# Batch 1's queries in one piece of 1024 rows, the first quarter's last links in halves with PSUM banks of their own, and a new order of all steps

## The chip, the core and the metric

The kernel runs on one core of a Trainium2 chip. A core has a matrix engine (PE, with its weight loads shown as PEld), a vector engine (DVE), a scalar engine (ACT), a general engine (POOL) and SP, which here only issues DMAs. Each engine works through its own queue in order. On-chip memory is SBUF (128 partitions) and PSUM, the matrix engine's output memory: eight banks of 512 float32 per partition. The metric is the time of one execution in device microseconds.

## The reference

Four batches of four heads, 1088 rows, head width 32; all inputs float32 except for the sketch matrices and the weights, which come as float64 words.

```python
phi(x) = outer(S1 x, S2 x)                     # 8 x 8 = 64 features per row and head
kv = phi(k)^T v ;  z = sum over rows of phi(k)
x  = (phi(q) kv) / (phi(q) z + 1e-6)           # attention, 4352 x 128 after the heads are joined
a, b = x @ w1, x @ w2                          # 128 -> 1024
out = ((a * b) @ w3) @ w_out                   # 1024 -> 1024 -> 128
```

The last two products are folded: the kernel forms w3 @ w_out (1024 x 128) once and applies that.

## The kernel before

**Steps and an order written out by hand.** `make_steps` defines 964 named steps, each a few instructions on one engine. The string `ORDER` lists all of them, and the last loop of the kernel runs them in that order and chains every engine's instructions (and all DMAs) to it. So each engine's queue is ORDER, cut down to that engine. `POOL` and `ACTS` name the steps that go to POOL or ACT; those in neither run on DVE where the step has a choice. `SLOTS` gives the buffer that each new tile takes: all PSUM tiles come from eight banks of kind "b", and raw weights from three buffers "raw" of 8 KB per partition.

**Keys** (steps `k0` to `k3`, one per batch). `load`, `loadr` bring a batch of k in (the last 64 rows apart), `max`, `g` find a scale, `lead` and `rest` split k into a leading part and the rest (L176/L177 on ACT or L179 on DVE, L600), `gram0` to `gram4` multiply (L608), and from the Gram matrix come `Gm`, `Gt`, `Ga`, `Gb`, `T0`, `T1`, `Ta`, `Tb`, `Ts`, `N0`, `N1`, `Na`, `Nb`, small steps on PE and DVE in turn. `N` gives the coefficients that the queries of the batch need. `ab`, `kp`, `kv`, `kq` form phi(k) and the batch's kv matrix.

**Queries.** `q0` and `q1` are the two halves of batch 0 (`q_part`; `q0` is the first quarter, kind "A"), `q2`, `q3` the halves of batch 1 (`q_wide` with 512 rows), `q4` and `q6` whole batches 2 and 3 (`q_wide` with 1024 rows), `qr` the last 64 rows of all batches. `q_wide` goes: `tr`, `max`, `l2`, `l1`, `rm` (transpose and split), `C0`, `A0`, `C1` on PE into four PSUM banks (L1303, L1294), `At`, `Ct` back to SBUF, then `sm`, `st`, `sh`, `sl`, `sc`, `al`, `p01`, `p2`, `p12`, `dn`, `de`, `rc` for the denominators, `bs`, `phi`, `pT`, then `x` on PE (L1417, four banks) and `xT`. A piece of 512 rows takes phi and pT from buffers of their own; a piece of 1024 takes them from two of the three "raw" buffers, which raw weights use too. In `q_part` of kind "A" the last links come in halves: `x0`, `x1` on PE, `xs0`, `xs1` on DVE, `xt0`, `xt1` on PE, `xT0`, `xT1` on ACT.

**Weights.** `w0`, `w1` bring w1 and w2 (two blocks of 512 columns), `w2` w_out, `w3` to `w10` the eight blocks of w3. Each goes load, `c`, `m` (ACT), `j` (DVE), `a0`, `a1` (POOL, L447 or L444). `f0` to `f7` fold a block of w3 into w_out: `t` on DVE, `m` on PE (L480), `o` on ACT.

**The two big products.** For each of eight groups `g` of 512 rows and each chunk `c` of 128 columns: `a` (L1458) and `b` (L1468) on PE, `c` copies a on ACT, `m` multiplies on DVE, `o` (L1481) sums over the chunks on PE; `gr` is the group of the last rows. `oT` and `st` turn and store a group.

**Warm-ups.** 29 steps `warm0` to `warm28` are 72 matmuls on zeros (L223), placed by ORDER among the others; nobody reads what they write.

Of the kernel before, what the change touches and what calls it, by code (L numbers as in the profile page):

```python
# [54 lines left out]
    k0.Nf k0.Nh k0.Nl k0.kp1 k1.kp0 k1.kp1 k2.kp0 k2.kp1 k2.rest0 k3.kp0 k3.kp1 k3.rest0 q0.p01 q0.p12  # L55
    q0.p2 q0.sca q0.scy q1.phi q2.al q2.bs q2.p01 q2.p12 q2.p2 q2.sc q3.p01 q3.p12 q3.p2 q3.phi0 q3.sc
    q4.al q4.p01 q4.p12 q4.p2 q6.al q6.p01 q6.p12 q6.phi1 q6.sc qr.sc s.Pp s.blk s.blkh s.rest
# [26 lines left out]
q3.C0 q3.A0 q3.C1 g0.4m g1.5m k2.kT1 q3.Ct q3.At k1.kvc w9.c g0.1ab w4.a0 w2.a0 w2.a1 f0.m g1.6a q4.max g0.1am q2.p01
q2.p2 q2.p12 q2.dn w4.a1 q4.l2 g1.6c q2.de k2.Ta g1.1a q2.rc g0.1ba g1.1b kr1.ab g1.4a g1.1c q2.bs g1.4c g0.1bc w9.m
kr1.abc k1.kqt f1.t k2.Tb q2.phi0 g1.4b f1.m k2.Ts q2.pT0 g1.1m k1.kq q2.x0 w9.j k2.N0 k2.N1 q4.l1 f0.o g1.4m k2.kT0
q3.sm g1.0o q3.st q2.xT0 g1.6b g2.5a q3.sh k2.Na k2.Nr q3.sl g1.2b g2.5c f1.o w9.a0 q3.sc warm15 q3.p01 v2.zero k2.ab
g1.6m k2.Nb q3.al q3.p2 q4.rm v2.load w6.load q4.C0 q4.A0 q4.C1 g1.2m k2.abt g2.5b w6.m w6.c g2.7a q4.Ct g0.1bb warm14
w5.load w7.load g2.0a w5.c g2.7c w7.c q4.At g1.1o g2.2b w9.a1 q3.p12 g0.1bm w7.m q3.dn q3.de w6.j g2.5m q3.rc w7.j
q3.bs q3.phi0 w5.j g2.2a g2.3a q3.load k3.load v2.loadr k3.loadr g2.3c g2.2c w7.a0 k3.max f6.t q4.sm g2.2m q4.st  # L90
q3.pT0 w7.a1 g2.4a g2.0b g2.6a w8.load f6.m g2.6c g2.0c w8.c g1.3b g1.3m k3.g g2.4c g2.7b g0.0o f6.o w8.m w8.j w8.a0
w10.load g2.0m w8.a1 q3.x0 q3.xT0 w5.m f4.t f5.t g2.1a g1.6o warm11 g2.1c k3.lead0 g2.1b g2.3b w5.a0 w5.a1 g2.3m f2.t
g2.7m g2.4b f5.m kh3.load f5.o w10.m f2.m f2.o w10.c w6.a0 g3.6a q4.sh g3.3a g0.1o w6.a1 f3.t q6.tr w10.j f3.m g3.7a
k3.kT0 k2.kp1 g2.1m f4.m w10.a0 g3.3c g3.7c f3.o q4.sl g0.2o g0.6o warm27 g0.3o warm26 g0.5o q4.sc k3.rest0 k2.kp0
g2.4m q4.al q4.p01 q4.p2 kr1.kp k3.gram0 f4.o k3.gram1 k2.kv0 k2.kv3 k2.kv1 k2.kv2 k3.gram2 k2.kvr k3.gram3 w10.a1
k3.gram4 k3.kT1 k3.ab q4.p12 q4.dn q3.restT k2.kvc k2.kqt k2.kq g3.1a g2.0o g0.4o k3.Gm k3.abt v3.zero f7.t g2.6b
g2.6m f7.m k3.kp0 q4.de q4.rc qr.max q4.bs k3.Gt f7.o k3.Ga v3.load v3.loadr g3.2a g0.7o g1.3o g1.4o g2.4o k3.Gb g2.6o
q6.max g3.0a g2.5o g1.5o g1.2o q4.phi0 q4.phi1 k3.kp1 k3.kv0 g0.oT q4.pT0 k3.kv1 q6.l2 q6.l1 q4.pT1 g3.2c g3.1c g3.0c
q6.rm g3.6c qr.l2 k3.kv3 k3.kv2 k3.T0 k3.T1 k3.Ta k3.kvr q4.x0 q4.x1 k3.Tb k3.N0 k3.Ts k3.N1 k3.Na k3.kvc k3.Nb q4.xT0
q4.xT1 g3.3b g2.3o g2.2o q6.C0 k3.Nr q6.A0 q6.C1 q6.At q6.Ct q6.sm q6.st q6.sh q6.sl q6.sc q6.p01 q6.al g4.6a g4.6c  # L100
g2.1o g1.7o g3.4a g2.7o g5.1b g5.3a k3.kqt g5.1a g3.3m qr.l1 g3.4c g4.0a g3.7b g2.oT g4.0c g5.1c g5.1m q6.p2 g3.4b
g4.5a g3.4m qr.rm g5.2a q6.p12 q6.dn q6.de g3.1b g5.5a k3.kq g5.3c g4.5c g3.1m q6.rc g5.5c g5.5b g5.7a g5.0a g5.5m
q6.bs q6.phi0 g4.1a g3.5a g3.7m g1.oT q6.pT0 g4.1c g5.0c g5.6a g5.7c g5.2c g3.0b g3.6b q6.phi1 q6.pT1 g3.6m q6.x0
q6.x1 g5.4a g3.0m g5.6c q6.xT1 g7.5a g4.0b g5.7b g7.5c q6.xT0 g5.4c g4.0m g6.4a g6.4c qr.C0 qr.A0 qr.C1 qr.At qr.sm
g3.5c qr.st g3.0o g5.2b g4.2a qr.sh qr.sl qr.Ct qr.sc g3.2b g3.4o g3.5b qr.al g4.7a g6.7a qr.p01 g3.2m qr.p2 g6.7c
g4.2c g0.st g3.3o qr.p12 g6.6a g5.4b g3.1o g5.0b g4.7c g5.4m qr.dn g3.5m g5.0m g4.3a g6.5a g7.2a g7.6a qr.de g6.5c
g7.6c g3.6o g7.3a g5.7m qr.rc qr.bs g5.3b g3.2o g3.5o g4.7b g5.2m g7.3c g6.6c g5.3m g7.2c g6.0a g4.3c g5.6b g5.0o
g6.0b g3.7o g3.oT qr.phi0 g4.5b g6.7b g6.2a g6.0c g5.6m g4.5m g7.6b g5.1o g5.2o g7.6m g4.7m g5.4o qr.pT0 qr.x0 g5.3o
g5.5o g6.2c qr.xT0 g7.5b gr.7a gr.0a gr.6a gr.0c gr.7c g6.7m g3.st g6.0m g7.5m g4.6b g7.0a g4.6m gr.6c g4.1b g5.6o
gr.4a gr.4c gr.4b gr.4m g4.4b g4.4a g4.4c g7.0c c.act g7.0b gr.5a gr.5c gr.5b g7.0m g4.1m g4.4m gr.5m g4.2b g6.3b  # L110
g6.1b gr.7b gr.7m g4.0o g6.1a g6.1c g4.3b g6.1m g4.4o g6.3a g6.4b g6.4m g4.3m g6.5b g5.7o g5.oT g4.2m g7.4b g7.1a
g7.2b g6.3c g6.6b g6.6m g7.1b g4.1o g7.2m g6.3m gr.1a g7.3b g7.3m gr.3a gr.1c g7.1c g4.2o g4.5o gr.6b g4.6o g4.3o
g4.7o g7.1m g4.oT g6.5m gr.2b g7.4a g6.2b gr.2a g7.4c g7.7a gr.2c gr.2m gr.0b gr.6m g6.2m g7.4m gr.3c g4.st g5.st
# [1465 lines left out]
```

## Time and profile before

| what | value |
|---|---|
| median of 3 runs | 252.19 us (252.1 to 252.4) |
| the profiled execution | 252.42 us, of which its span is 250.5 us |
| PE busy | 245.4 us, 98% of the span |
| DVE busy | 160.0 us (64%), 9 tenths or more in most slices up to 100 us |
| ACT, POOL busy | 100.2 us, 82.0 us |
| granted PE clock | 9 tenths or more in every slice |

All times below are microseconds from the start of the profiled execution's span. The busy share of PE counts the warm-up matmuls too. A matmul of float32 is two records. Durations overlap, since matmuls are pipelined: what a matmul costs the queue is the distance from its start to the next one's, not its own length (a 128x512 matmul record is 0.59 us long, and the next starts 0.43 us after it).

### The profile page before, as it was taken

To read this page: it belongs to the slowest core of one execution; us is meant where nothing else is said; L and a number is where in the kernel's file an instruction comes from. 1 tells how busy PE (TensorE), PEld (TensorE's weight loads), DVE (VectorE), ACT (ScalarE), POOL (GpSimd) and SP (SyncE) were. 2 spreads that over 40 slices of the span, in tenths; PEclk is the share of its full clock that TensorE was granted. 3 is DMA by queue.
4 is the path that set the end of the run, shared out by engine and by line. 5 is a ranking of instruction groups with operands and counts; after the bars stand their busy time and mean duration, and the time that the engine had idled before them with its cause. 6 is when DMAs were issued, how large, how long until landed. Compare 5 with 4: busy or idle time off the path is not lost.

```text
span 250.5 us, 6030 instructions
## 1 busy us (share of the span) xinstructions
PE 245.4 (98%) x2511; PEld 139.9 (56%) x2511; DVE 160.0 (64%) x351; ACT 100.2 (40%) x186; POOL 82.0 (33%) x111
## 2 busy tenths in 40 slices
...
GB/s 184 183 193 329 270 166 175 211 238 237 137 270 235 129 86 0 3 33 61 39 5 3 0 0 4 1 0 3 0 35 7 3 0 0 0 0 84 22 106 63
DMA packets 31131, 22.02 MB, mean 88 GB/s; under 512 B 21248, under 2 KB 25600, under 8 KB 30976
## 3 DMA queue, kind: packets, MB, share of 16 engines
...
q10 hardware_dynamic: 688, 0.59, 0.8%
q8 instruction: 20, 0.33, 0.6%
...
## 4 chain that ended last, share of the span: by engine, by line
PE 92%; DVE 3%; DMA 2%; issue 1%; SPq 1%
PE a_ps L1458 24%; PE b_ps L1468 24%; PE ps_o L1481 22%; PE ps_w3o L480 6%; PE ps_g L608 3%; PE ps_x L1417 2%; PE ps_ac L1303 2%; DMA qh<-in_q_dram 2%; PE ps_kv L718 2%; PE ps_or L1488 1%; PE idle_ps L223 1%; PE ps_xt L1199 1%; PE ps_ab L676 1%; DVE k_m L182 1%; PE ps_kq L754 0%
## 5 line engine op out<-in xcount | busy, mean ns | idle before, releaser
L1474 DVE TENSOR_TENSOR ab<-ffa,b_ps 128x512 f32<-128x512 f32 (+1 forms) x74 | 45.9, 636 | 44.3 <-PE b_ps L1468 34.7
L1463 ACT COPY ffa<-a_ps 128x512 f32<-128x512 f32 (+1 forms) x74 | 38.6, 555 | 86.6 <-PE a_ps L1458 80.9
L1468 PE MATMUL b_ps<-xT,w 128*128 128x512 f32 (+1 forms) x148 | 67.4, 560 | 0.0
L1458 PE MATMUL a_ps<-xT,w 128*128 128x512 f32 (+1 forms) x148 | 66.8, 561 | 0.0
L1481 PE MATMUL ps_o<-ab,w3o 128*128 128x512 f32 x128 | 60.9, 595 | 0.0
L1468 PEld LDWEIGHTS b_ps<-xT,w 128*128 128x128 f32 x148 | 27.4, 190 | 27.9 <-issue 23.4
L1458 PEld LDWEIGHTS a_ps<-xT,w 128*128 128x128 f32 x148 | 27.1, 190 | 27.6 <-issue 22.1
L1481 PEld LDWEIGHTS ps_o<-ab,w3o 128*128 128x128 f32 x128 | 23.8, 190 | 26.0 <-issue 24.3
L444 POOL TENSOR_TENSOR w3c<-cv_c,cv_m 128x512 int32<-128x512 int32 x16 | 20.3, 1281 | 12.5 <-DVE cv_c L433 8.8
L1497 DVE STREAM_TRANSPOSE oT<-ps_o 128x512 f32<-128x512 f32 x8 | 5.7, 713 | 18.7 <-PE ps_o L1481 18.7
L480 PEld LDWEIGHTS ps_w3o<-wo,w3T 128*128 128x128 f32 x128 | 15.4, 192 | 2.9 <-issue 2.2
L480 PE MATMUL ps_w3o<-wo,w3T 128*128 128x128 f32 x128 | 15.4, 275 | 0.0
L1350 POOL TENSOR_TENSOR s_hl<-s_hl,ay_C 128x256 f32<-128x256 f32 (+2 forms) x4 | 3.2, 794 | 37.1 <-DVE s_hl L1346 25.8
L223 PE MATMUL idle_ps<-zeros 128*128 128x256 bf16 x72 | 12.9, 312 | 1.0 <-DVE zeros L195 1.0
L419 ACT ACTIVATE cv_m<-raw 128x1024 int32<-128x1024 uint32 x11 | 13.1, 1188 | 0.0
L231 ACT ACTIVATE cv_c<-raw 128x1024 f32<-128x1024 f32 x11 | 12.9, 1185 | 0.0
L626 POOL TENSOR_TENSOR kp<-kabt 128x1024 f32<-128x1024 f32 x6 | 12.1, 2024 | 1.9 <-DVE kabt L694 1.2
L474 DVE STREAM_TRANSPOSE w3T<-w3c 128x1024 f32<-128x1024 f32 x8 | 9.8, 1223 | 1.0 <-POOL w3c L444 1.0
L223 PEld LDWEIGHTS <-zeros 128*128 128x128 bf16 x72 | 7.8, 111 | 4.0 <-issue 1.3
L1398 POOL TENSOR_TENSOR ph<-s_al,s_bs 128x1024 f32<-128x1024 f32 x2 | 5.1, 2560 | 9.2 <-DVE s_bs L1388 9.2
L1428 ACT COPY xT<-ps_x 128x128 f32<-128x128 f32 (+2 forms) x20 | 4.7, 323 | 8.6 <-PE ps_x L1417 8.6
L608 PE MATMUL ps_g<-kk 128*32 128x64 f32 x288 | 7.8, 224 | 0.2 <-DVE kk L600 0.2
...
## 6 DMA issues: line engine op xcount, KB each, us to landing
...
```

Source lines behind the costliest of these rows:

```text
L223: pe.matmul(t, zeros, bview(zeros, [[0, 2], [1, 128]]), start=True, stop=True)
L231: act.activation(dst, hi.bitcast(F32), ACT.Prelu, scale=2.0 ** -112, alpha=-2.0 ** 32)
L419: act.mul(x["m"], words(0).bitcast(U32), 2.0 ** -29)
L444: pool.tensor_tensor(d, c, m, ALU.add)
L480: pe.matmul(t["o"], w3T[ko][:, c], wo[:, c], start=c == 0, stop=c == NC - 1)
L608: pe.matmul(o[h * D:(h + 1) * D], lhs, rhs, start=start, stop=stop, skip_group_check=True)
L626: eng.tensor_mul(dst, bview(av, [list(av.ap[1]), list(av.ap[2]), [0, r]]), bview(bv, [list(bv.ap[1]), [0, r], list(bv.ap[2])]))
L1458: pe.matmul(x["a"][:, :w], w_of(0, c), xT[g][:, c0:c0 + w], start=True, stop=True)
L1463: act.copy(x["s"][:, :w], x["a"][:, :w])
L1468: pe.matmul(x["b"][:, :w], w_of(1, c), xT[g][:, c0:c0 + w], start=True, stop=True)
L1474: dve.tensor_mul(ab_sb[g, c][:, c0:c0 + w], x["s"][:, :w], x["b"][:, :w])
L1481: pe.matmul(o_ps[g], w3o[:, c], ab_sb[g, c], start=c == 0, stop=c == NC - 1)
```

## The change

Batch 1's queries are one piece of 1024 rows: the steps of `q3` go, those of `q2` work on twice the columns and get second halves (`phi1`, `pT1`, `x1`, `xT1`). So `q2`'s phi and pT now sit in two of the three "raw" buffers. In `q_part` of kind "A", the halves of `x` and of `xt` get a PSUM tile each instead of sharing one. ORDER, POOL and SLOTS are new throughout. 32 steps change between DVE and POOL, among them `q1.phi`, `k3.kp0`, `k3.kp1`, `k0.Nf` to DVE and `q0.phi1`, `q0.al`, `q1.p01`, `q1.p2`, `q1.p12`, `q4.phi0`, `q4.phi1` to POOL. The diff, with ORDER up to batch 2's Gram matmuls and its end, and without POOL and most of SLOTS:

```diff
 SLOTS = {
...
-    "raw": "012101021010210",
+    "raw": "01210120120120120",
...
 ORDER = """
-c.zeros c.ident s.load s.four warm13 k0.zero warm12 warm10 warm9 warm7 k0.load0 k0.loadr k0.load1 q0.load k2.zero
-c.mask s.words k0.max0 kr0.load k0.max1 s.pair k0.max2 s.lead s.low k0.g k0.lead0 warm1 k0.tr1 k0.tr0 warm0 s.sum
-k0.lead1 q0.tr kr0.tr s.rest warm18 k0.rest0 s.T s.tc k0.gram0 s.R k0.gram1 k0.rest1 k0.gram2 k0.gram3 k0.gram4 s.zero
-s.c s.blkh s.blk k1.zero q0.max s.P warm22 q1.tr q0.l2 k0.Gm k0.Gt k0.kT0 k0.Ga k0.Gb w1.load k2.loadr q0.l1 s.Pc
-k0.T0 s.Pm q1.max q0.restT k0.T1 q0.rm k0.Ta kr0.kT k0.kT1 warm4 warm3 k0.ab0 q0.A0 k0.ab1 k0.Tb kr0.ab s.Pp k1.load
-k1.loadr k0.Ts q0.C0 k0.abc0 k0.kp0 k0.N0 k0.N1 k1.max warm24 k0.abc1 q0.sma k0.kp1 k1.tr1 k0.Na k0.Nh kr0.abc k1.tr0
-q1.l2 k1.g v0.zero v0.load warm2 q0.sta k0.Nb k0.Nl q0.sha q0.C0t k1.kT1 q1.l1 q0.A1 k0.kv0 k0.kv3 k0.Nf q0.C1 k0.kv1
-v0.loadr k0.kv2 kr0.kp q0.smy q0.sla k1.lead0 q0.sty q1.rm kr1.load q0.shy k0.kvr warm21 q0.sca q0.p01 q0.al q1.C0
-q0.sly q0.C1t k0.kvm q0.phi0 k0.Nr k0.kzt k2.load q0.phi1 k1.kT0 k0.kz q0.pt0 k1.rest0 q1.A0 warm8 q1.sm kr1.tr q0.pc0
-q0.pt1 w0.load q0.x0 q0.pc1 w0.c q1.st q0.scy q0.p2 q0.p12 s.RC q1.load q0.dn q0.x1 q1.sh q0.de w0.j q0.rc k1.gram0
-q0.xs0 q0.xs1 k1.gram1 k1.gram2 k1.gram3 w0.m q1.sl k1.gram4 warm19 k1.Gm k0.kvc q0.xt0 q1.restT q1.sca k2.max w0.a0
-q0.xt1 w0.a1 warm16 q1.p01 q1.scy k1.Gt warm5 warm17 warm6 s.AR q1.al q1.p2 q1.p12 q1.dn w1.c q0.xT0 q1.de g0.0aa
-q0.xT1 g0.3a g0.2a kr1.kT g0.2c g0.0ac w1.m g0.3c w2.load s.KS k1.Ga k2.g w1.j g0.3b g0.0ab w1.a0 g0.2b g0.0ba k1.T0
-k1.Gb k1.T1 k1.ab q1.rc q1.bs g0.0bc k0.kqt k2.lead0 q3.tr g0.0am g0.2m k1.abt k1.Ta g0.0bb g0.7a g0.4a q1.phi g0.4c
-g0.7c k1.Tb k1.Ts q3.max g0.3m w1.a1 g0.5a q1.pt0 q1.pt1 g0.5b g0.6a k2.rest0 q3.l2 q3.l1 g0.5c q2.tr q2.max q2.l2
-g0.6c q1.pc0 k1.N0 k1.N1 k2.gram0 k2.gram1 k2.gram2 k2.gram3 k1.kp1 k1.kp0 q1.pc1 k2.gram4 warm23 k1.Na g0.5m w3.load
...
-gr.1b g7.4o g2.st g7.2o gr.1m g7.7m gr.3m g7.3o g7.1o g7.7o gr.0o1 gr.6o1 gr.6o0 gr.5o0 g7.oT gr.1o0 gr.5o1 gr.1o1
-gr.4o1 gr.3o1 gr.2o1 g7.st gr.7o1 gr.4o0 gr.3o0 gr.2o0 gr.7o0 gr.oT0 gr.oT1 gr.st1 gr.st0 warm25 warm20 warm28
+c.mask k2.zero c.ident k0.zero s.load c.zeros k0.loadr k0.load0 k0.load1 k0.max0 warm0 k0.tr1 k0.max1 warm14 warm13
+s.words s.pair warm7 warm19 q0.load s.lead warm10 warm1 warm3 k0.max2 s.low k0.g s.sum s.rest k0.lead0 k0.lead1 warm4
+s.P s.T s.tc q0.restT q1.tr k0.rest0 k0.rest1 s.four k0.gram0 k0.gram1 k0.gram2 k0.gram3 k0.gram4 q0.tr q0.max s.Pm
+k0.Gm s.R s.c s.Pc k0.Gt k0.Ga s.blk k0.Gb k0.tr0 k0.kT0 q0.l2 q1.max warm2 k0.T0 kr0.load k0.T1 k0.Ta q0.l1 k0.kT1
+k0.ab0 k0.abc0 k1.zero s.zero s.blkh kr0.tr v0.zero s.Pp w1.load k2.loadr kr0.kT q1.l2 warm22 k0.Tb k0.Ts k1.load
+k0.N0 k0.N1 q0.rm k0.Na q0.A0 k0.ab1 q0.C0 v0.load k0.kp0 k1.tr0 k0.Nh k0.abc1 q1.l1 q0.A1 k1.kT0 q0.C0t q0.sma
+v0.loadr k1.loadr warm23 warm17 kr0.ab k0.kp1 k1.tr1 warm15 q0.sta kr1.load warm16 k0.kv0 k1.max k0.kv3 q0.sha kr0.abc
+k0.Nb kr0.kp k1.g k0.Nf q0.sla k2.load w0.load k0.kv1 k0.kv2 k0.Nl k0.kvr q0.C1 q0.sca k1.kT1 k1.lead0 q1.rm q0.al
+q0.smy k0.kvm q1.A0 q1.C0 s.KS q0.C1t q0.sty q0.phi0 q0.pt0 q1.sm q0.phi1 warm18 warm26 warm8 k0.kzt q0.pt1 kr1.tr
+q0.pc0 q0.shy k1.rest0 k0.kz q0.x0 w0.c k1.gram0 k1.gram1 k1.gram2 k1.gram3 k1.gram4 q1.st q0.pc1 q0.sly q0.p01 q0.scy
+q1.sh q0.p2 w0.j warm27 q1.load k0.kvc q1.sl q0.p12 k0.Nr q0.x1 kr1.kT w0.m w0.a0 q0.dn q0.de q0.rc q0.xs0 q0.xs1
+q0.xt0 q0.xT0 warm12 warm9 q0.xt1 g0.1aa w0.a1 g0.0aa k2.max q0.xT1 w1.c g0.2a g0.2b g0.0ab q1.sca k2.g k1.Gm k1.Gt
+g0.0ac g0.1ac w1.m warm24 q2.tr g0.1ba q1.p01 w2.load warm21 w1.j w3.load k1.Ga warm5 q1.al v1.zero w1.a0 k1.T0 k1.Gb
+q1.scy q1.p2 q1.p12 k1.T1 k1.ab g0.2c q1.restT g0.2m warm6 k1.abt k2.lead0 g0.1bc g0.0bb k1.Ta k1.Tb q2.max g0.7a
+q2.load w1.a1 g0.7c q1.dn g0.0am w3.c q1.de s.RC k2.rest0 g0.5a g0.0ba g0.3a g0.6a g0.3c g0.0bc k2.gram0 q2.l2 g0.6c
+q2.l1 k2.gram1 k1.Ts q1.rc q1.bs k2.gram2 k2.gram3 k2.gram4 k1.N0 k1.N1 q1.phi q1.pt0 q1.pt1 w3.j k3.zero g0.0bm
...
+g7.oT g5.st gr.5o1 gr.4m gr.3b gr.1o1 gr.4o1 gr.6o0 g6.oT g7.st gr.5o0 gr.3m gr.7m gr.2m gr.1o0 gr.4o0 gr.3o1 g6.st
+gr.2o1 gr.7o1 gr.3o0 gr.2o0 gr.7o0 gr.oT0 c.act gr.oT1 gr.st0 warm28 gr.st1 warm11 warm20
...
                 @step(nm(f"x{u}"))
                 def _(u=u):
-                    if u == 0:
-                        s["x"] = ps("h", [128, nj, H * D], "ps_xt")
-                    o = s["x"]
+                    s["x", u] = o = ps("h", [128, 2, H * D], "ps_xt")
                     for j in range(2 * u, 2 * u + 2):
                         for p in range(2):
-                            pe.matmul(o[:, j, 64 * p:64 * (p + 1)], s["pT"][:, p, j * 128:(j + 1) * 128],
+                            pe.matmul(o[:, j - 2 * u, 64 * p:64 * (p + 1)], s["pT"][:, p, j * 128:(j + 1) * 128],
                                       kz[b][:, 64 * p:64 * (p + 1)], start=True, stop=True)
...
                 @step(nm(f"xt{u}"))
                 def _(u=u):
-                    if u == 0:
-                        s["xp"] = ps("t", [128, 512], "ps_xs")[:, :n]
-                    for j in range(2 * u, 2 * u + 2):
-                        pe.transpose(cols(s["xp"], j), s["xs"][:, j], ident)
+                    s["xp", u] = ps("t", [128, 256], "ps_xs")
+                    for j in range(2):
+                        pe.transpose(cols(s["xp", u], j), s["xs"][:, 2 * u + j], ident)
...
...
         if g < 2:
             q_part(g, b, half * 512, 512, "AL"[g])
-        elif b < 2:
+        elif b < 1:
             q_wide(g, b, half * 512, 512, lambda t, g=g: (g, t * 128))
         elif half == 0:
             q_wide(g, b, 0, 1024, lambda t, g=g: (g + t // 2, t % 2 * 256))
```

101 lines of the change are left out of this document (50 added, 51 removed).

## The prediction

> **What bounds the kernel now.** I read the page's table of engines first, then who waited for whom on PE, then the busy time by stage, then the order of time of single stretches.
>
> ```profile
> PE 245.4 (98%) x2511; PEld 139.9 (56%) x2511; DVE 160.0 (64%) x351; ACT 100.2 (40%) x186; POOL 82.0 (33%) x111
> ```
>
> The list of PE's waits, in full (total, times, longest):
>
> ```profile
> PE idle_ps L223 <- DVE zeros L195: 1.0, 1, 1.0
> PE ps_kv L718 <- DVE s_bs L989: 0.6, 1, 0.6
> PE ps_T L822 <- DVE G_a L172: 0.3, 1, 0.3
> PE ps_g L608 <- DVE kk L600: 0.2, 1, 0.2
> ```
>
> The stages, in microseconds: PE, PEld, DVE, ACT, POOL, clock, DMA share, GB/s.
>
> ```profile
> 0.00:10.00 10.00, 8.85 (x119) 7.06 (x121) 5.94 (x17) 4.66 (x11) 3.26 (x35) 1.00 0.67 196
> 10.00:20.00 10.00, 8.86 (x235) 7.73 (x227) 9.28 (x34) 6.67 (x14) 5.92 (x13) 1.00 0.66 177
> 20.00:30.00 10.00, 10.00 (x266) 9.42 (x256) 9.86 (x24) 7.72 (x14) 7.61 (x10) 1.00 0.91 324
> 30.00:40.00 10.00, 10.00 (x69) 5.56 (x68) 9.59 (x32) 7.46 (x11) 6.38 (x4) 1.00 0.77 192
> ```
>
> PE loses time only in the first 20 us. From there to the last output matmul it is one queue without a gap. So the time is: where PE stands at some point after the front, plus the PE work queued behind that point, plus the tail. DVE is 93 to 99% busy from 10 to 40 us, so the front is set by DVE's chain as much as by PE.
>
> **The PE work.** Batch 1's two pieces and one wide piece, by order of time on PE: `q2.C0`, `A0`, `C1` and the next matmul, then the same of `q6`, then `q6.x0`, `x1` and the next.
>
> ```profile
> 45.95 0.50 PE L1303 MATMUL ps_ac<-qT,RC 32*32 32x128 f32 x32
> 46.38 0.27 PE L1294 MATMUL ps_ac<-q,AR 64*32 64x128 bf16 x8
> 46.58 0.50 PE L1303 MATMUL ps_ac<-q,RC 32*32 32x128 f32 x32
> 47.02 1.55 PE L1458 MATMUL a_ps<-xT,w 128*128 128x512 f32 x3
> ...
> 131.36 0.71 PE L1303 MATMUL ps_ac<-qT,RC 32*32 32x256 f32 x32
> 132.00 0.33 PE L1294 MATMUL ps_ac<-q,AR 64*32 64x256 bf16 x8
> 132.25 0.72 PE L1303 MATMUL ps_ac<-q,RC 32*32 32x256 f32 x32
> 132.90 0.70 PE L1458 MATMUL a_ps<-xT,w 128*128 128x512 f32 x1
> ...
> 153.06 1.79 PE L1417 MATMUL ps_x<-pT,kq 32*32 32x256 f32 x64
> 154.78 0.70 PE L1458 MATMUL a_ps<-xT,w 128*128 128x512 f32 x1
> ```
>
> A narrow piece costs 47.02 - 45.95 = 1.07 us here and 1.10 for `q3`, and its `x` 0.86 and 1.00 (starts of 64 matmuls to the next one's): 4.03 us in all. A wide piece costs 1.54 and 1.72: 3.26. Saved: 0.75 us; with `q4`'s 1.62 in place of 1.54, 0.7. PE changes between small tiles and full 128x128 ones 18 times in both orders, so that cost stays. Of the 72 warm-up matmuls 3 stood behind the last output matmul and 4 do now: 0.11 us less in the way. PE work: **-0.8 us**. The PSUM halves add and remove no instruction. In the kernel before `xs0` ran 0.9 us after `x1` had ended, so the shared tile made nobody wait: 0. DVE and POOL also lose instructions, about 2 and 1 us in sum, but after 105 us both idle for long, and that is worth nothing there.
>
> **The front.** PE's queue up to batch 2's Gram matmuls (`k2.gram0`, 41.19 before) now holds less: `g0.3b`, `g0.4a`, `g0.5b` (2.58), `q1.pt0`, `pt1` (0.9), `k0.kqt`, `k1.N0`, `N1` (0.5) went behind it, `g0.1aa`, `g0.1ba` (0.86) came ahead; 0.65 us of warm-ups came ahead too. With the 0.8 saved, the work behind `k2.gram0` grows by 1.7 to 1.8 us. So the kernel is faster if `k2.gram0` starts before 41.2 - 1.75 = 39.4. Two chains set that start.
>
> First, group 0's first matmul (29.20 before). `k1.loadr` is now issued behind `v0.load` and `v0.loadr` on SP, and `k1.max` on DVE needs it. `v0.load` takes over k0's buffer, free after `k0.tr0` at about 11.8; four issues of 0.4 to 0.8 later `k1.loadr` goes out at 13.3, and rows of 32 KB land 4 to 5.7 us behind their issue (DMA list: 5.7, 4.8, 4.4): 17.3 to 19. DVE is there at about 17.2 (it ran `k1.max` at 16.13 without a wait). I take 17.7, near the low end, since the queue had stretches with a DMA share of 0.2 there. What waits behind it on DVE: `q0.sha`, `k0.Nb`, `k1.g`, and through them `k1.lead0` on ACT, `k0.Nl` on POOL and `q0.C1` on PE. From `k1.max` to `q0.xs0` DVE has 27 steps, 9.9 us by their own rows of before; so `xs0` ends at 27.9 (27.60 before). Transposes, ACT's copy (0.37) and three handovers bring `g0.1aa` at 28.9, bounds 28.2 (no wait at `k1.max`) and 30.2 (landing at 19). PE then has 9.3 us of work to `k2.gram0`: arrival 38.2.
>
> Second, `k2.rest0` on POOL. After `q0.xT1` (29.5) ACT does `w1.c` 1.15, two copies 0.55, `w1.m` 1.1, `g0.2c`, `k2.lead0` 2.4: end 35.2. POOL waits for `w1.m` (32.3), then does `w1.a0` 1.25, `q1.p2`, `q1.p12` (0.4 each, now on POOL), `w1.a1` 1.25, `s.RC` 0.5 (was 10 us earlier): 36.1; `k2.rest0` 2.64 ends at 38.75, and the Gram matmuls start at 38.9. This is the later one. PE waits 0.7 us there that it did not wait before.
>
> ```profile
> 36.78 1.27 POOL L447 TENSOR_TENSOR w<-w,cv_m 128x512 int32<-128x512 int32 x1
> 38.00 2.64 POOL L600 TENSOR_TENSOR kk<-k,kk 128x1152 f32<-128x1152 f32 x1
> ...
> 37.32 0.77 DVE L854 TENSOR_TENSOR T_p<-T_p 32x32 f32<-32x32 f32 x1
> ```
>
> In these rows DVE's `k1.Ts` (32 numbers a partition; 0.18 for the same step of the other batches) lasted 0.77 and ended at 38.09, as POOL's addition ended (38.05): it stood still while POOL worked. The longest step of this sort is `q4.sc`, 3.00 us on DVE beside POOL's `k3.rest0` of 3.08, against 1.27 for `q6.sc` alone on POOL. The Trainium skill, "SBUF — State Buffer", section "SBUF: two separate sides", gives the rule: a DVE operation with two SBUF inputs and a GpSimd operation that reads SBUF share one pair of ports, and whichever starts first keeps the other out for its whole length. The trace agrees by these rows; by the rule the new `q1.phi` on DVE, two SBUF inputs, could go in front of `k2.rest0`, which is the second rival below.
>
> **The tail.** `c.act`, a copy of one element (0.18 at 202.30), now stands between `gr.oT0` and the store that ACT issues: 0 to 0.2, I take 0.1. `g6.st` now comes last on SP, ahead of `gr.st1`; it ends its issues about when `gr.oT1` is ready: 0.
>
> **The sum.** 38.9 - 41.2 + 1.75 + 0.1 = -0.45. The profiled execution took 252.42: 251.97; it is 0.23 above the median of 252.19, so **251.7** on that scale. Two times of this kernel can be told apart from about 0.2%, 0.5 us, on.
>
> **The rivals.**
> - *The front is free* (no wait at `k1.max`, `k2.rest0` in 2.2 to 2.6 us): Gram at 37.9 to 38.4, 250.8 to 251.2. For: DMA's short idle stretches. Against: five POOL steps more ahead of `k2.rest0`.
> - *`k2.rest0` comes late, slower.* Place: POOL ahead of `k2.gram0`. `k3.rest0` took 3.08 (+0.45), and a two-input step of DVE that gets ahead (`q1.phi`, 1.2 us) pushes it by as much: 39.4 to 40.5, 252.2 to 253.3. It decides from 39.4 on. For: the rows above. Against: DVE reaches `q1.phi` at about 38, when `k2.rest0` already runs.
> - *A wait at `q4.C1`* (about 80 us). It needs `q4.rm`, which on DVE stands behind `g2.7m`, that behind ACT's `g2.7c`, and that behind `f1.o`, which needs the end of `f1.m`. Sum 0.15 + 0.27 + 0.58 + 0.1 + 1.3 + 1.2 to 1.75 + 0.2 = 3.8 to 4.4; PE has 4.1 us of work in between. Wait 0 to 0.3; together with a late ACT up to 1: 252.0 to 252.8.
> - *The clock.* The first 19 warm-ups start 0.213 us apart, as do the first transposes, and from 5.3 us on 0.11: PE starts at half speed. Now 16 warm-ups and then four transposes fill that time. Half speed for 2 to 4 us more (it lasted 4.3) would cost PE 1 to 2 us, about half of it hidden in the front's waits: 252.8. The Trainium skill, "TensorE: Matmul & The Clock Gate", "Part 1: The HAM clock gate" and "Part 4: PE-mode transpose", says that a window of activity of some 3.4 us opens the gate and that transposes do not count as activity; by that rule the opening could slip by one window. That transposes hold it back no row here shows, so its chance is small.
> - *Weights late.* `q2`'s phi and pT hold two raw buffers until about 67 us, so `w6`, `w7`, `w8` load later; `f3.m` follows their landing by over 15 us. Small, 252.8.
>
> **How the numbers follow.** The sum with its terms' bounds, 251.2 to 252.2: 0.45, of which 0.22 lies below 251.69. Front free 0.17. `k2.rest0` late 0.20, a quarter of it within 0.2%. `q4.C1` 0.11, clock and weights 0.07, all slower. Faster 0.39, same 0.28, slower 0.33. The range 250.9 to 253.2 leaves out the ends of the first and of the slower rivals.
>
> **What would show it.** `x1` and `C0` of batch 1 at 32x256 and PE's busy records down by 72 logical matmuls; `k1.max` starting at 17.2 to 19; the first L1458 matmul near 28.9; the next group of L608 matmuls behind it starting at 38.9, right behind the end of POOL's L600. It is wrong if PE shows idle time behind 45 us, or if the L608 start lies outside 38 to 39.4.

## The result, and the profile after

The changed kernel takes **253.66 us** (median of 6 executions, 253.22 to 254.46) against 252.22 us: a ratio of 1.0061, 95% interval 1.0044 to 1.0079. It is 1.44 us slower, where 0.5 us faster was forecast. The profiled execution took 253.83 us, 1.41 more than that of before; its span, from the first to the last instruction, is 251.6 us, 1.0 more (250.55 to 251.56). The remaining 0.4 lies outside the span, where single executions of the changed kernel scatter between 1.7 and 2.9 us; nothing in the trace shows what it is. Single executions of some kernels took 2 to 3% longer than the others of the same kernel, at a lower granted clock; medians and ratios here leave them out.

The page's table of engines and the full list of PE's waits (total, times, longest), after:

```profile
PE 246.0 (98%) x2375; PEld 139.1 (55%) x2375; DVE 160.6 (64%) x331; ACT 99.7 (40%) x180; POOL 84.4 (34%) x109
```

```profile
PE ps_xs L1214 <- DVE xs L1206: 1.4, 1, 1.4
PE idle_ps L222 <- DVE zeros L194: 1.0, 1, 1.0
PE ps_g L607 <- POOL kk L599: 0.2, 1, 0.2
PE ps_g L607 <- DVE kk L599: 0.2, 1, 0.2
```

The second line is the first warm-up, as before. The waits at `ps_kv` (0.6) and for `G_a` (0.3) are gone; in their place PE waits 1.4 us for `xs0`, a DVE step of the first quarter, and a little for `k2.rest0` on POOL. The stages (PE, PEld, DVE, ACT, POOL, clock, DMA share, GB/s):

```profile
10.00:20.00 10.00, 9.96 (x255) 8.40 (x247) 9.39 (x34) 6.50 (x15) 5.65 (x11) 1.00 0.78 235
20.00:30.00 10.00, 8.62 (x217) 8.00 (x207) 9.68 (x23) 6.71 (x12) 7.73 (x7) 1.00 0.76 265
30.00:40.00 10.00, 9.84 (x72) 5.52 (x73) 9.11 (x26) 8.86 (x15) 7.71 (x11) 1.00 0.76 189
```

From 10 to 20 us PE is now fuller than before (9.96 against 8.86). What it loses, it loses between 20 and 30 us (8.62 against 10.00). From 40 us on it has no gap. So three terms make up the difference in the span, as the prediction set it up: where `k2.gram0` starts, the PE work behind it, and the tail. By order of time on PE, group 0's first matmul and `k2.gram0`:

```profile
30.16 1.96 PE L1454 MATMUL a_ps<-xT,w 128*128 128x256 f32 x6
...
39.96 0.34 PE L607 MATMUL ps_g<-kk 128*32 128x64 f32 x8 [0.16 <-POOL kk L599]
```

| term (us) | before | after | difference | forecast |
|---|---|---|---|---|
| `k2.gram0` starts | 41.18 | 39.96 | -1.22 | -2.3 |
| from there to the start of the last output matmul | 205.82 | 207.95 | +2.13 | +1.75 |
| from there to the end of the span | 3.55 | 3.65 | +0.10 | +0.1 |
| sum | | | +1.0 | -0.45 |

The front came 1.06 us later than forecast, and PE has 0.38 us more work behind it. The front first. DVE and POOL by order of time, just ahead of `xs0`:

```profile
26.62 0.42 DVE L1119 TENSOR_REDUCE s_d<-s_pr 128x32 f32<-128x256 f32 x1
27.07 1.16 DVE L1124 SCALAR_TENSOR_TENSOR s_rc<-s_d 128x16 f32<-128x16 f32 x1
28.27 0.25 DVE L1128 RECIPROCAL s_rc<-s_rc 128x16 f32<-128x16 f32 x1
28.63 0.76 DVE L1206 TENSOR_TENSOR xs<-ps_xt,s_rc 128x256 f32<-128x256 f32 x2
```

```profile
25.80 0.78 POOL L1114 TENSOR_TENSOR s_pr<-s_pr 128x128 f32<-128x128 f32 x1 [0.95 <-DVE s_pr L1110]
26.94 2.48 POOL L446 TENSOR_TENSOR w<-w,cv_m 128x512 int32<-128x512 int32 x2 [0.36 <-ACT cv_m L418]
...
36.80 0.50 POOL L344 COPY RC<-Sc 128x32 f32<-128x32 f32 x3
37.26 2.64 POOL L599 TENSOR_TENSOR kk<-k,kk 128x1152 f32<-128x1152 f32 x1
```

The DVE line of 1.16 us is `q0.de`, an addition of 16 numbers a partition. In the kernel before, the same step took 0.17:

```profile
26.14 0.17 DVE L1125 SCALAR_TENSOR_TENSOR s_rc<-s_d 128x16 f32<-128x16 f32 x1
```

In the changed kernel it starts 0.13 us after POOL has begun the first weight addition `w0.a0` (a single one lasts 1.27, so it runs from 26.94 to 28.21) and ends at 28.23, with it. That is 0.99 us in the chain to `xs0`, and everything behind is late by 1.0 to 1.15: ACT's `w1.m` ends at 33.32 (forecast 32.3), `k2.lead0` at 36.25 (35.2), `k2.rest0` at 39.90 (38.75). Whether this is the cause, and not merely what it looks like, is for the experiments.

### The profile page after: what moved, and what is told of

The parts are those of the page before. It is cut to its first block, busy times and chain, and to the rows that moved or that the text cites. A ratio compares the mean times of both kernels' runs of the same rounds, so it can differ in the third digit from the quotient of the medians.

```text
span 251.6 us, 5738 instructions
## 1 busy us (share of the span) xinstructions
PE 246.0 (98%) x2375; PEld 139.1 (55%) x2375; DVE 160.6 (64%) x331; ACT 99.7 (40%) x180; POOL 84.4 (34%) x109
## 4 chain that ended last, share of the span: by engine, by line
PE 86%; DVE 7%; POOL 3%; DMA 2%; SPq 1%; issue 1%; POOLq 0%; DVEq 0%
PE b_ps L1464 23%; PE ps_o L1477 22%; PE a_ps L1454 21%; PE ps_w3o L479 6%; PE ps_x L1413 2%; PE ps_g L607 2%; PE ps_ac L1299 2%; DMA qh<-in_q_dram 2%; PE ps_or L1484 1%; PE ps_kv L717 1%; DVE k_m L181 1%; POOL kk L599 1%; PE ps_ab L650 1%; DVE kk L599 1%; PE idle_ps L222 1%; DVE w L432 1%
## 5 line engine op out<-in xcount | busy, mean ns | idle before, releaser
L1470 DVE TENSOR_TENSOR ab<-ffa,b_ps 128x512 f32<-128x512 f32 (+1 forms) x74 | 44.7, 632 | 51.6 <-PE b_ps L1464 48.4
L1459 ACT COPY ffa<-a_ps 128x512 f32<-128x512 f32 (+1 forms) x74 | 39.2, 555 | 82.2 <-PE a_ps L1454 82.0
L1464 PEld LDWEIGHTS b_ps<-xT,w 128*128 128x128 f32 x148 | 27.4, 190 | 29.8 <-issue 25.0
L443 POOL TENSOR_TENSOR w3c<-cv_c,cv_m 128x512 int32<-128x512 int32 x16 | 21.6, 1365 | 13.3 <-DVE cv_c L432 9.6
L1394 POOL TENSOR_TENSOR ph<-s_al,s_bs 128x1024 f32<-128x1024 f32 (+1 forms) x7 | 13.6, 1969 | 2.6 <-DVE s_bs L1384 2.5
L222 PE MATMUL idle_ps<-zeros 128*128 128x256 bf16 x72 | 11.9, 306 | 1.0 <-DVE zeros L194 1.0
L1346 POOL TENSOR_TENSOR s_hl<-s_hl,ay_C 128x512 f32<-128x512 f32 x2 | 2.5, 1270 | 26.9 <-DVE s_hl L1342 26.2
L1424 ACT COPY xT<-ps_x 128x256 f32<-128x256 f32 (+1 forms) x16 | 4.4, 359 | 15.7 <-PE ps_x L1413 15.7
L625 POOL TENSOR_TENSOR kp<-kabt 128x1024 f32<-128x1024 f32 x4 | 7.8, 1947 | 5.7 <-DVE kabt L693 5.7
L1384 POOL TENSOR_TENSOR s_bs<-ay_C,s_rc 128x256 f32<-128x256 f32 (+1 forms) x3 | 1.6, 520 | 23.3 <-DVE s_rc L1379 19.1
```

What stands on the lines that cost most here:

```text
L222: pe.matmul(t, zeros, bview(zeros, [[0, 2], [1, 128]]), start=True, stop=True)
L443: pool.tensor_tensor(d, c, m, ALU.add)
L1394: on(nm(f"phi{u}")).tensor_mul(x, bview(s["al"][:, u * g], [[r, g], [1, r], [0, r]]), bview(s["bs"][:, u * g], [[r, g], [0, r], [1, r]]))
L1459: act.copy(x["s"][:, :w], x["a"][:, :w])
L1464: pe.matmul(x["b"][:, :w], w_of(1, c), xT[g][:, c0:c0 + w], start=True, stop=True)
L1470: dve.tensor_mul(ab_sb[g, c][:, c0:c0 + w], x["s"][:, :w], x["b"][:, :w])
```

## The experiments

Times of each kernel. The kernel before, measured beside them, took 252.29 us beside `e1` to `e4`, 252.22 beside `changed`, `e5`, `e6`, `e7` and `e8`, and 252.41 beside `e9`, `e10` and `e12`. The start of `k2.gram0` is counted from the first matmul of `k0.gram0`, since that first matmul itself comes at 8.7 to 9.4 us in different executions; the last column is from `k2.gram0` to the end of the span. `e3_both`, the changed kernel with two small edits, is the one that `e7` and `e12` start from; `e10` starts from `e7`.

| kernel | us | ratio to before | `k2.gram0` | rest |
|---|---|---|---|---|
| before | 252.22 | | 32.47 | 209.4 |
| changed | 253.66 | 1.0061 [1.0044, 1.0079] | 31.28 | 211.6 |
| e1_fill | 252.66 | 1.0017 [1.0002, 1.0032] | 30.30 | 211.7 |
| e2_rc | 253.53 | 1.0047 [1.0029, 1.0065] | 30.83 | 211.5 |
| e3_both | 252.44 | 1.0007 [0.9990, 1.0024] | 29.81 | 211.4 |
| e4_w1c | 252.62 | 1.0014 [1.0000, 1.0028] | 30.14 | 211.4 |
| e7_x | 252.07 | 0.9989 [0.9973, 1.0005] | 29.89 | 211.0 |
| e12_halves | 252.66 | 1.0014 [1.0000, 1.0028] | 30.02 | 211.5 |
| e10_pe | 251.36 | 0.9958 [0.9943, 0.9974] | 29.52 | 211.0 |
| e6_mend | 257.43 | 1.0204 [1.0189, 1.0219] | 34.4 | 211.4 |
| e9_pool | 257.45 | 1.0211 [1.0188, 1.0235] | 29.26 | 217.0 |
| e8_split | 260.74 | 1.0338 [1.0289, 1.0387] | 30.95 | 219.2 |
| e5_halves | 254.20 (two executions) | 1.0076 [1.0057, 1.0095] | | |

### Let `q0.de` go first: more work on POOL

```diff
+    @step("s.fill")
+    def _():
+        pool.memset(w12[:, 1].rearrange("p i c -> p (i c)")[:, :640], 0.0)
...
-q1.sh q0.p2 w0.j warm27 q1.load k0.kvc q1.sl q0.p12 k0.Nr q0.x1 kr1.kT w0.m w0.a0 q0.dn q0.de q0.rc q0.xs0 q0.xs1
+q1.sh q0.p2 w0.j warm27 q1.load k0.kvc q1.sl q0.p12 k0.Nr q0.x1 kr1.kT w0.m s.fill w0.a0 q0.dn q0.de q0.rc q0.xs0
```

> The changed kernel with one more operation on POOL, right ahead of the first weight addition w0.a0: a memset of 640 numbers a partition in a buffer that is written later anyway (nothing reads the zeros). In the changed kernel w0.a0 starts at 26.94 and q0.de on DVE at 27.07; q0.de lasts 1.16 us instead of 0.17 and ends with w0.a0. Theory: q0.de is shut out by the POOL addition that began first. The memset (about 0.6 us) lets q0.de go first: it lasts 0.2, xs0 and the first matmul of group 0 come 1.0 us earlier (30.16 to about 29.2), k2.rest0 ends 1.0 earlier, the Gram matmuls of batch 2 start at 38.9 to 39.0 instead of 39.96, and the kernel takes 252.6 to 252.8 us although POOL has 0.6 us more work in the way. Rival one, DVE's chain to xs0 is simply longer, in the new order, than the sum of its steps said: q0.de is then late for another reason, xs0 comes when it came, and the memset costs 0 to 0.6: 253.6 to 254.3. Rival two, the POOL chain alone sets the Gram matmuls: 0.6 more on POOL moves k2.rest0 later or not at all: 253.6 to 254.3.

DVE and POOL of this kernel, in order of time:

```profile
27.34 0.17 DVE L1128 SCALAR_TENSOR_TENSOR s_rc<-s_d 128x16 f32<-128x16 f32 x1
...
26.80 0.63 POOL L343 MEMSET w<- 128x640 f32 x1
27.39 2.50 POOL L450 TENSOR_TENSOR w<-w,cv_m 128x512 int32<-128x512 int32 x2
```

With 0.63 us more work on POOL in the way of the weights, `q0.de` takes 0.17 us again, `k2.gram0` starts 0.98 us earlier, and the kernel is 1.0 us faster. The intervals of the two ratios do not overlap. The theory gave 252.6 to 252.8; both rivals gave 253.6 or more and fall.

### The copies ahead of `k2.rest0`

```diff
-q1.sh q0.p2 w0.j warm27 q1.load k0.kvc q1.sl q0.p12 k0.Nr ...
+q1.sh q0.p2 w0.j warm27 q1.load k0.kvc q1.sl s.RC q0.p12 k0.Nr ...
-q2.load w1.a1 g0.7c q1.dn g0.0am w3.c q1.de s.RC k2.rest0 ...
+q2.load w1.a1 g0.7c q1.dn g0.0am w3.c q1.de k2.rest0 ...
```

> The changed kernel with s.RC (three copies, 0.50 us) moved from right ahead of k2.rest0 into POOL's idle time ahead of q0.p12 (24.85 to 25.80). Theory: q0.de is still shut out, the first matmul of group 0 stays at 30.16, and PE arrives at the Gram matmuls at 39.63; k2.rest0 ends 0.46 earlier, so PE's wait of 0.33 there goes and no more: 253.2 to 253.4. Rival two, the POOL chain alone sets the Gram matmuls and what is ahead of it does not matter: the full 0.46, start at 39.5, 253.1 to 253.2; told from the theory by whether PE waits at all at the Gram matmuls afterwards. Rival one makes no difference here.

`q0.de` on DVE, `k2.rest0` on POOL, and PE's only wait at Gram matmuls, which is at those of batch 1, for DVE's `k1.rest0`:

```profile
27.22 1.10 DVE L1124 SCALAR_TENSOR_TENSOR s_rc<-s_d 128x16 f32<-128x16 f32 x1
...
36.90 2.64 POOL L599 TENSOR_TENSOR kk<-k,kk 128x1152 f32<-128x1152 f32 x1
```

```profile
PE ps_g L607 <- DVE kk L599: 0.4, 1, 0.4
```

`q0.de` is still shut out, and the wait for POOL's `kk` has left the list: `k2.rest0` ends at 39.54, and PE comes to `k2.gram0` at 39.81. Counted from group 0's first matmul (30.25) it comes 0.24 earlier than in the changed kernel, not the 0.46 by which POOL's work ahead shrank. So PE's arrival decides there, as the theory had it. The span is 0.3 shorter; the median, 253.53, lies just outside the 253.2 to 253.4 expected and does not tell the kernel from the changed one.

### Both, and another way to the same end

> Both of the two edits before: the memset ahead of w0.a0, and s.RC in POOL's idle time ahead of q0.p12. Theory: the two terms add up as far as PE's arrival lets them: group 0's first matmul at 29.2, PE arrives at the Gram matmuls at about 38.6, k2.rest0 ends at 38.4, start 38.6 to 38.8: 252.2 to 252.5, as fast as the kernel before. Rival one (DVE's chain is long in itself): as s.RC alone, 253.2 to 253.9.

252.44 us, within 0.1% of the kernel before; `k2.gram0` 1.47 us earlier than in the changed kernel (1.2 to 1.4 were expected). The two terms, 0.98 and 0.45, add up.

The fourth kernel delays `w0.a0` without a memset, by what ACT does ahead of it:

```diff
-... q1.sl q0.p12 k0.Nr q0.x1 kr1.kT w0.m w0.a0 q0.dn ...
+... q1.sl s.RC q0.p12 k0.Nr q0.x1 kr1.kT w1.c w0.m w0.a0 q0.dn ...
```

> The changed kernel with s.RC in POOL's idle time ahead of q0.p12 and w1.c (1.15 us on ACT) moved ahead of w0.m, into time in which ACT waits; there is no memset. ACT then ends w0.m about 1.1 us later and POOL starts w0.a0 at 28.0 instead of 26.94, so q0.de goes first. Theory: q0.de lasts 0.2, xs0 comes 1.0 earlier, but group 0's first matmul now also waits for w0.a0, which ends at 29.3: it starts at 29.4 instead of 30.16; the Gram matmuls start at 38.8 to 39.0: 252.4 to 252.7. Rival one: the later w0.a0 costs and nothing is gained: 253.3 to 254.

```profile
27.23 0.17 DVE L1124 SCALAR_TENSOR_TENSOR s_rc<-s_d 128x16 f32<-128x16 f32 x1
...
28.05 2.49 POOL L446 TENSOR_TENSOR w<-w,cv_m 128x512 int32<-128x512 int32 x2 [1.31 <-ACT cv_m L418]
```

The weights come 1.1 us later than in the changed kernel, `q0.de` takes 0.17, group 0 starts at 29.38 and the kernel takes 252.62, all as expected. It is not the memset that helps but which of the two engines starts first.

### What the wide piece saved on PE

```diff
+        pieces = [slice(0, W // 2), slice(W // 2, W)] if b == 1 else [slice(0, W)]
...
-                    pe.matmul(ac[h][t * 32:(t + 1) * 32, :W], RC[rows, bof(t), x].rearrange("p f i -> p (f i)"),
-                              quarter(src, t)[rows], start=start, stop=not start, tile_position=(h * D, t * 32),
+                        pe.matmul(ac[h][t * 32:(t + 1) * 32, c], RC[rows, bof(t), x].rearrange("p f i -> p (f i)"),
+                                  quarter(src, t)[rows, c], start=start and c.start == 0, stop=not start,
```

(and `A0`, `x` in the same way)

> The changed kernel with each matmul of batch 1's C0, A0, C1, x0 and x1 cut into two of half the columns (32x128 again instead of 32x256), in the order of two narrow pieces, and nothing else: the cost on PE of two narrow pieces at the place of the wide one. The prediction priced the merge at 0.7 to 0.75 us of PE work; by that term the kernel gets 0.7 to 0.75 slower (254.3 to 254.4, C0 to C1 from 1.65 to 2.17 and x0 with x1 from 2.00 to 2.2). Rival, from the steps in the trace of the changed kernel: C0 to C1 saved 0.5 and x next to nothing, since k2.N0 and k2.N1 now stand ahead of x0 and between x0 and x1; the kernel gets 0.5 slower (254.1 to 254.2) and x stays at 2.0 to 2.1.

`C0`, `A0`, `C1` and the next matmul on PE, of the changed kernel and then of this one:

```profile
46.27 0.82 PE L1299 MATMUL ps_ac<-qT,RC 32*32 32x256 f32 x32
47.02 0.30 PE L1290 MATMUL ps_ac<-q,AR 64*32 64x256 bf16 x8
47.25 0.73 PE L1299 MATMUL ps_ac<-q,RC 32*32 32x256 f32 x32
47.92 0.70 PE L1454 MATMUL a_ps<-xT,w 128*128 128x512 f32 x1
```

```profile
46.68 1.09 PE L1303 MATMUL ps_ac<-qT,RC 32*32 32x128 f32 x64
47.71 0.31 PE L1293 MATMUL ps_ac<-q,AR 64*32 64x128 bf16 x16
47.94 1.07 PE L1303 MATMUL ps_ac<-q,RC 32*32 32x128 f32 x64
48.94 1.13 PE L1459 MATMUL a_ps<-xT,w 128*128 128x512 f32 x2
```

Wide costs 1.65, cut in two 2.26: the merge saves 0.6 us there. `x0` with `x1`, `k2.N0` and `k2.N1` included, costs 2.17 cut in two against 2.15: nothing. The whole time, 260.74 us, says something else and cannot be set against either number. PE stood still in the middle of a product:

```profile
54.84 3.55 PE L1459 MATMUL a_ps<-xT,w 128*128 128x512 f32 x4 [3.92 <-issue]
```

```profile
52.00:54.00 2.00, 0.00 (x0) 0.00 (x0) 1.75 (x3) 0.00 (x0) 0.70 (x1) 1.00 1.07 238
...
56.00:58.00 2.00, 2.00 (x3) 0.68 (x2) 0.00 (x0) 0.00 (x0) 0.00 (x0) 0.50 0.63 149
```

It waited for nothing that the profile records, while the DMA engines were full (share 1.07), and afterwards its clock was at half for some 3 us. This kernel has 136 more PE records, and its instruction queue carried 20 packets against 18. That PE's next instructions, which have a DMA queue of their own, came late behind the weights fits this; it was not tested.

### Keep the small tiles together

```diff
-q2.phi0 f0.m kh2.load q3.load g1.3c g0.6b w5.c g1.4m q2.pT0 g1.0m f0.o k2.Ts q2.restT q2.phi1 q2.pT1 g0.6m k2.N0
-k2.kT1 q2.x0 k2.N1 q2.x1 q2.xT0 g1.3b ...
+q2.phi0 f0.m kh2.load q3.load g1.3c g0.6b w5.c g1.4m q2.pT0 g1.0m f0.o k2.Ts q2.restT q2.phi1 q2.pT1 g0.6m
+k2.kT1 q2.x0 q2.x1 k2.N0 k2.N1 q2.xT0 g1.3b ...
```

> The kernel with the memset ahead of w0.a0 and s.RC in POOL's idle time (252.44 us), and with k2.N0 and k2.N1 moved behind q2.x1 on PE, so that x0 and x1 are one run of 64 matmuls as in q6. Theory: the two steps that stood ahead and between cost x 0.27 us; x0 with x1 takes 1.72 instead of 2.00: 252.1 to 252.3. Rival: the cost of going between small and full tiles only moves to k2.N0 and k2.N1, which cost 0.27 instead of 0.15, and the time falls by 0.1 or not at all: 252.3 to 252.5.

From the first of these matmuls to the next product, in the changed kernel (`k2.N0`, L859, then `x`, with `k2.N1`, L865, inside) and here:

```profile
67.96 0.22 PE L859 MATMUL ps_N<-T_p,P2a 32*32 32x16 f32 x4
...
70.11 1.13 PE L1464 MATMUL b_ps<-xT,w 128*128 128x512 f32 x2
```

```profile
66.89 1.56 PE L1417 MATMUL ps_x<-pT,kq 32*32 32x256 f32 x56
...
68.61 1.13 PE L1468 MATMUL b_ps<-xT,w 128*128 128x512 f32 x2
```

2.15 us became 1.72, and 0.43 less lies behind `k2.gram0` (211.4 to 211.0): more than the theory's 0.27, because, counted by starts, `N0` and `N1` at the end of the run cost 0.51 in place of 0.15, but `x` only 1.21 in place of 2.00. The median fell by 0.37; the intervals overlap, so it is the trace that carries this. That `N1`, issued in the middle, held up `x1` until `x0` had left the tiles that it needs, is argued from the order, not shown.

### The PSUM halves undone

```diff
-                    s["x", u] = o = ps("h", [128, 2, H * D], "ps_xt")
+                    if u == 0:
+                        s["x"] = ps("h", [128, nj, H * D], "ps_xt")
+                    s["x", u] = o = s["x"][:, 2 * u:2 * u + 2]
...
-                    s["xp", u] = ps("t", [128, 256], "ps_xs")
+                    if u == 0:
+                        s["xp"] = ps("t", [128, 512], "ps_xs")
+                    s["xp", u] = s["xp"][:, 256 * u:256 * u + 256]
```

> The changed kernel with the PSUM halves undone: x0 and x1 of the first quarter share one bank again, and xt0 and xt1 share one; every other tile keeps its bank. Theory: 0, as predicted, since x1 has ended (at 27.5) before xs0 starts (28.6), and xt1 follows xt0 by 0.5 us, before ACT's copy of the first half starts or as it does: 253.5 to 253.8. Rival: with one bank xt1 or xT0 waits for the other half, 0.3 to 0.4 us: group 0's first matmul later by that, 253.9 to 254.1.

Two executions of this kernel count, 254.18 and 254.23, just above the rival's 253.9 to 254.1; its profile does not. Two are few, so the edit was repeated on a kernel whose front is not held up by `q0.de`:

> The kernel with the memset ahead of w0.a0 and s.RC in POOL's idle time (252.44 us), with the PSUM halves undone: x0 and x1 share one bank, xt0 and xt1 share one, every other tile keeps its bank. In the run of the same edit on the changed kernel, xt1 on PE started at 30.12, right behind ACT's copy xT0 (29.70 to 30.07), instead of 0.24 us ahead of its end as before: in the new order xT0 stands ahead of xt1. Theory now: the halves are worth that wait, 0.2 to 0.4 us: xt1 starts at 29.15 instead of 28.94, group 0's first matmul at 29.5 instead of 29.22: 252.6 to 252.8. Rival, the prediction's own term: 0, 252.3 to 252.5.

ACT's two copies `xT0`, `xT1` and PE's `xt1` between them:

```profile
29.04 0.37 ACT L1226 COPY xT<-ps_xs 128x256 f32<-128x256 f32 x1 [1.93 <-PE ps_xs L1222]
29.94 0.37 ACT L1226 COPY xT<-ps_xs 128x256 f32<-128x256 f32 x1 [0.53 <-PE ps_xs L1222]
...
29.46 0.44 PE L1222 MATMUL ps_xs<-ident,xs 128*128 128x128 f32 x2
```

`xt1` now starts 0.90 us behind `xt0` instead of 0.68, once the copy of the first half has ended (29.41). `k2.gram0` starts 0.21 later and the median is 0.22 higher. The intervals overlap, so it is the trace that carries this: the halves are worth 0.2 us in this order, in which `xT0` stands ahead of `xt1`. In the order before, both `xt` stood ahead of both copies, and PE's list of waits shows none for a shared bank.

### A version to beat both

There were three tries. The first moved DVE's steps of `q1` behind `xs1`, `w1.c` and `w1.j` ahead, `s.RC` too, and eight warm-up matmuls to the end:

```diff
-... q1.st q0.pc1 q0.sly q0.p01 q0.scy q1.sh q0.p2 w0.j warm27 q1.load k0.kvc q1.sl q0.p12 k0.Nr q0.x1 kr1.kT w0.m w0.a0
+... q0.pc1 q0.sly q0.p01 q0.scy q0.p2 w0.j warm27 q1.load k0.kvc s.RC q0.p12 k0.Nr q0.x1 kr1.kT w0.m w1.c w0.a0
-q0.dn q0.de q0.rc q0.xs0 q0.xs1 ... k2.max ...
+q0.dn q0.de q0.rc q0.xs0 q0.xs1 w1.j q1.st q1.sh q1.sl ... q1.sca k2.max ...
```

> A version to beat both kernels: the changed kernel with s.RC in POOL's idle time ahead of q0.p12; q1.st, q1.sh, q1.sl on DVE moved behind q0.xs1, so that q0.p2, q0.p12, q0.dn and q0.de come 0.7 to 1.0 us earlier and q0.de runs before w0.a0 starts; w1.c on ACT ahead of q0.xT0, in its waiting time; w1.j and q1.sca on DVE ahead of k2.max; and eight warm-up matmuls (0.9 us) that stood between q0.xt0 and g0.7a moved behind the last output matmul. Theory: group 0's first matmul at 28.5 to 28.8, k2.rest0 ends by 37.6, the Gram matmuls at 37.5 to 37.9 instead of 39.96: 251.2 to 251.7. Rival: a PSUM bank that q1.st, q1.sl hold longer makes PE wait, or k2.rest0 stays at 38.5: 252.3 or more.

It took 257.43 us. The longest wait of PE, and DVE's `w1.j` and `k2.g` ahead of it:

```profile
PE ps_T L821 <- DVE G_a L171: 3.3, 1, 3.3
```

```profile
28.62 1.78 DVE L432 TENSOR_SCALAR w<-cv_c 128x1024 int32<-128x1024 int32 x1
...
33.27 1.36 DVE L587 TENSOR_TENSOR k_g<-k_m,grid 128x2 f32<-128x2 f32 x1
```

`w1.j` began while `w0.a1` was running (to 29.85) and took 1.78 instead of 0.83 in the changed kernel; `k2.g` met `w1.a0` (33.36 to 34.61) and took 1.36 instead of 0.15. With these and the steps put ahead of it, `k1.Ga` came at 36.04 (33.07 in the changed kernel), PE idled 3.34 us at `k1.T0`, and its clock was at half from 38 to about 41.

The second try leaves DVE's order alone. It takes the kernel with the memset, `s.RC` and the grouped `x`, groups batch 2's `x` and `k3.N0`, `k3.N1` too, and clears PE's way:

```diff
-q0.xt0 q0.xT0 warm12 warm9 q0.xt1 ... warm24 ... warm21 ... warm5 ... warm6 ... warm25 ...
+q0.xt0 q0.xT0 q0.xt1 ...
-... g1.5o k3.N0 k3.N1 q4.x0 q4.x1 ...
+... g1.5o q4.x0 q4.x1 k3.N0 k3.N1 ...
-... gr.oT0 c.act gr.oT1 gr.st0 warm28 gr.st1 warm11 warm20
+... gr.oT0 gr.oT1 gr.st0 warm28 warm12 warm9 warm24 warm21 warm5 warm6 warm25 gr.st1 warm11 warm20
```

> The kernel of 252.07 us (memset ahead of w0.a0, s.RC in POOL's idle time, k2.N0 and k2.N1 behind q2.x1), with the same done for batch 2 (k3.N0 and k3.N1 behind q4.x1), nine warm-up matmuls that stood in PE's queue behind q0.xt0 moved behind the last output matmul (0.95 us), and c.act moved off the end. Theory: PE arrives at the Gram matmuls of batch 2 at about 37.9 but k2.rest0 ends at 38.5, so of the eight warm-ups ahead of them only 0.2 is gained; the one behind them is worth 0.1, q4's x 0.1 to 0.4, c.act 0.1: 251.3 to 251.7. Rival: the warm-ups were worth their time because the clock falls without them, 252.5 or more.

It took **251.36 us**, ratio 0.9958 (0.9943 to 0.9974): faster than both kernels, by about 1.1 us than the one before. `k2.gram0` starts 0.29 earlier than in the kernel with memset and `s.RC`. Behind it the 0.43 of `q2`'s grouping stays and nothing is added: `q4`'s `x` with `k3.N0` and `k3.N1` fell from 1.85 to 1.73, but the stretch as a whole (211.0) is no shorter, so this, the warm-up and `c.act` were worth nothing that shows there. These two terms make 0.7 us against `e3_both`; the rest of its gain, 0.3 to 0.5 us, lies ahead of `k0.gram0` or outside the span and is not explained.

The third try also moved `q2.tr` behind `w1.j` and `w1.c` ahead of `q0.xT0`, to have `k2.rest0` earlier:

> The same, and POOL's chain to k2.rest0 cut too: q2.tr on DVE (1.24 us) moved from ahead of w1.j to right ahead of q2.max, and w1.c on ACT moved ahead of q0.xT0 into time in which ACT waits. Theory: w1.a0 starts at 31.4 instead of 32.4, k2.rest0 ends at 37.3 to 37.8 and the Gram matmuls start at 37.9 instead of 38.8: 250.6 to 251.2. Rival: a DVE or POOL step that now starts while the other engine's two-input step runs is shut out for its length (w1.j beside q1.p01, 0.7), and the gain over the kernel without these two moves is 0.3 or nothing: 251.2 to 251.8.

It took 257.45 us. `k2.rest0` ended at 38.36 and `k2.gram0` started 0.26 earlier than in the second try: little came of it. Behind it, DVE met POOL three times in a row (`w3.j`, `s.AR`, `k1.Nr`):

```profile
41.17 2.44 DVE L436 TENSOR_SCALAR cv_c<-cv_c 128x1024 int32<-128x1024 int32 x1
...
44.32 1.31 DVE L352 TENSOR_TENSOR AR<-Sc,mask2n 128x64 bf16<-128x64 f32 x1
45.56 1.93 DVE L895 TENSOR_TENSOR AR<-RC,mask2n 128x16 bf16<-128x16 f32 x1
```

```profile
40.59 2.47 POOL L629 TENSOR_TENSOR kp<-kabt 128x1024 f32<-128x1024 f32 x1
44.28 1.28 POOL L447 TENSOR_TENSOR w3c<-cv_c,cv_m 128x512 int32<-128x512 int32 x1 [1.22 <-DVE N_t L168]
45.51 1.95 POOL L629 TENSOR_TENSOR kp<-kabt 128x1024 f32<-128x1024 f32 x1
```

5.68 us for steps that take 1.06 in the changed kernel (0.69, 0.21, 0.16). PE waited 3.3 us at `q2.C0`, and its clock fell to half. In kind that was the rival; in size it was far worse than the 251.2 to 251.8 the rival named.

## Why the prediction was wrong, point by point

- **The frame held.** PE is one queue; the time is the start of `k2.gram0`, the work behind it and the tail. The tail's 0.1 came as forecast, and there is no wait behind 45 us, so the rivals at `q4.C1` and with late weights did not occur. Nor did the clock slip at the start: PE's matmuls stand 0.11 us apart from 4.8 us on, in the kernel before from 5.6 (the prediction read 5.3).
- **The front's first chain is where it failed**, in the sentence "From `k1.max` to `q0.xs0` DVE has 27 steps, 9.9 us by their own rows of before". `k1.max` came at 17.36 without a wait, 0.34 ahead of the 17.7 taken, which hid part of the miss: from there to the end of `xs0` 11.69 us passed instead of 10.2. For the rows of before hold the lengths that those steps had beside the POOL work of before. `q0.de` took 1.16 instead of 0.17, since `w0.a0` started 0.13 us ahead of it. The next largest is `q0.shy`, 0.82 instead of 0.55: it began inside `q0.phi1` (21.27 to 22.84), one of the steps that the change moved to POOL. With `q0.de` alone put right, in e1, the same stretch takes 10.50. `xs0` ended at 29.05 instead of 27.9 and group 0 began at 30.16 instead of 28.9. That this is inside the bound of 30.2 is luck, since the bound was for a late landing of `k1.loadr`. PE arrived at `k2.gram0` at 39.6 (39.20, the start of its last matmul ahead, plus 0.43) instead of 38.2, so that it waited 0.3 there instead of the 0.7 forecast.
- **The second chain was right in its lengths and wrong in its start.** `k2.rest0` took the 2.64 forecast and was the later of the two, but ended 1.15 late, because `w1.c` on ACT stands behind `q0.xT1` and that behind `xs0`. In the e1 kernel it ends at 39.18; counted from `k0.gram0`, that is 0.97 earlier than in the changed kernel and 0.2 behind the forecast.
- **The rival had the mechanism and not the place.** That POOL's additions shut DVE out was in the text, with `k1.Ts` and `q4.sc` as rows and the rule of the Trainium skill, "SBUF — State Buffer", "SBUF: two separate sides", beside it. The trace agrees with that rule for the steps with two SBUF inputs shown here: each stretched one began inside a POOL operation with two inputs (`k2.g` 0.09 us ahead of one) and ended within 0.15 us of that operation's end, or, like `q4.sc` (0.56), less than one own length later. The prediction applied it to `q1.phi` against `k2.rest0` only. That `k2.gram0`, at 39.96, came inside the 39.4 to 40.5 of this rival, and outside the 38 to 39.4 that the forecast allowed itself, is therefore no hit: it was `q0.de`, in the other chain, that made it late. Every DVE step of that chain should have been laid against POOL's new times. `q0.de` and `w0.a0` began 0.13 us apart, far closer than a forecast with bounds 2 us apart for group 0 can tell, so their meeting belonged among the rivals.
- **PE work: -0.8 forecast, about -0.4 came.** `C0` to `C1` saved 0.5 to 0.6, as forecast (0.6). `x` saved nothing, 2.00 against 1.86 for the two narrow ones: it was priced from `q6`, which runs alone, and here `k2.N0` and `k2.N1` stand ahead of it and inside it; grouped, it costs 1.72 with `N0` and `N1` included. Another 0.12 was lost at `q4`, whose `x` now runs behind `k3.N0` and `k3.N1` instead of ahead of them (1.85 against 1.73 for the four steps).
- **PSUM halves: 0 forecast, a gain of 0.2 by the trace of e12.** The argument looked at the order before only.
